# A causal convolution in 64x32 TensorE tiles, eight at once, with a band read as a Toeplitz matrix from one line of taps

## The chip, the cores and the metric

One core of one Trainium2 chip. The metric is the device time of one execution in microseconds, the median of several runs. Each run carries a state, since executions can be slower when the granted clock is lower.

## The reference

A lightweight convolution (eight heads of 24 channels, seven taps each, causal) over 8 x 4160 tokens of 192 channels, then a maxout feed-forward layer:

```python
w = softmax(weight)                              # 8 heads x 7 taps
out[b, s, h, :] = sum_k w[h, k] * x_pad[b, s + k, h, :]      # 6 zero rows ahead of x
h = maximum(maximum(out @ w1, out @ w2), out @ w3)           # 192 -> 768
y = h @ w_out                                                # 768 -> 192
```

## The kernel before

The convolution runs on TensorE. For a chunk of tokens and a head, x (tokens on partitions, 32 channels) is the stationary operand, and a band matrix of the head's taps moves past it. The tokens are cut in 65 blocks of 512; block 64 consists of the eight last 64 tokens of the sequences. Convolutions run four blocks ahead of the feed-forward layer (L285 is its first layer, L319 its second). All code below is cut; `...` marks it.

```python
BAND_W = 128 + PAD        # PAD = 6
CHK = P - PAD             # 122 output tokens from 128 rows

def load_x(t):            # SyncE; consecutive full chunks go in one DMA
    ...
        nc.sync.dma_start(out=xf[0:rlen0, i:k + 1, :], in_=src)

# band: zeros to DRAM, taps scattered over a diagonal, read back, then transposed by two copies
nc.scalar.dma_start(out=Rd[:], in_=zero[:])
...                       # exp, sum, reciprocal, 7 multiplies on 128 partitions
nc.scalar.dma_start(out=bass.AP(... ap=[[BW + NHEAD, P], [1, KW * NHEAD]]), in_=taps...)
nc.scalar.dma_start(out=bandc..., in_=Rd[:])
...
def conv(t):
    for (q, b, row_lo, rlen, lo, hi, cc) in chunks_of[t]:
        for h in range(NHEAD):
            g = h % 4
            ...
            nc.tensor.matmul(G[h // 4][32 * g:32 * g + 32, lo:hi],
                lhsT=x16[0:rlen, q, cb:cb + 32], rhs=band[0:rlen, h, cc:cc + hi - lo],
                start=True, stop=True, tile_position=(0, 32 * g))
...
for t in range(AHEAD):    # start-up: four blocks
    conv(t); evac(t, 0); evac(t, 1)
    repack(t)             # 24-channel heads to dense rows: 10 or 20 small DMAs
    load_x(t + 3); cast_x(t + 3); double(t)   # (under conditions, cut)
    ...
```

The softmax here doesn't subtract the row's maximum and nothing guards it: scores larger than these inputs give would overflow.

## Time and profile before

| | before |
|---|---|
| median (3 runs) | 514.97 us (514.89 to 515.39) |
| span of the profiled run | 513.0 us |
| first, second, fifth, sixth convolution start | 24.68, 26.65, 46.30, 54.36 us |
| period of the loop, from one convolution to the next | 7.046 us |
| first to last matmul of a full block's convolution | 476 ns, 40 pairs of weight load and matmul |

Two more matter afterwards. The first is from the page's list of DMA queues (packets, megabytes, share of the DMA engines' time), the second from its groups of instructions (count, busy us and mean ns, then idle time just before the group and what ended it):

```profile
q8 instruction: 70, 1.15, 1.0%
...
L285 PE MATMUL lq<-yd,wd 64*128 64x512 f16 x1170 | 317.3, 378 | 0.4 <-DVE h L290 0.3
```

The reader sees 70 packets of 16 KB (1.15 MB / 70) that carry instructions, and a first layer that waits 0.4 us in all. TensorE executes 8906 loads and 8906 matmuls, so one packet stands for about 17,812 / 70 = 254 of them.

### The profile page before, as it was taken

How to read it: one execution, taken by the hardware profiler on the slowest of the kernel's cores; microseconds unless marked ns; L12 is line 12 of the kernel's file. 1: busy time of each engine (PE TensorE's matmuls, PEld its weight loads, DVE VectorE, ACT ScalarE, POOL GpSimd, SP SyncE). 2: the span in 40 equal slices, each digit the busy share in tenths (PEclk: the TensorE clock that was granted, in tenths of full speed). 3: DMA queues.
4: the chain of work that ended last, by engine and by line, in shares of the span. 5: the costliest groups of instructions: out<-in, count | busy, mean ns of one | idle time of the engine just before them, and what ended most of it. 6: DMA issues, size and time to landing. Idle time of an engine off the chain costs nothing.

```text
span 513.0 us, 21247 instructions
## 1 busy us (share of the span) xinstructions
PE 470.8 (92%) x8906; PEld 322.7 (63%) x8906; DVE 335.4 (65%) x542; ACT 355.6 (69%) x654; POOL 143.4 (28%) x205
## 2 busy tenths in 40 slices
PE   0084999999999999999999999999999999999993
PEld 0082666666666666666666666666666666666893
DVE  1321676767776777777677767677776777676772
ACT  1132777777777777777777777777777777777661
POOL 1131322333223323223332233322233322323213
PEclk9996999999999999999999999999999999999998
DMA  7825566777666666677666666666677766655412
GB/s 176 215 78 133 139 195 194 198 190 196 176 178 168 186 170 181 186 196 194 194 178 186 188 183 162 171 185 181 195 202 194 190 175 192 172 148 145 123 66 63
DMA packets 65752, 87.72 MB, mean 171 GB/s; under 512 B 7593, under 2 KB 51305, under 8 KB 65657
## 3 DMA queue, kind: packets, MB, share of 16 engines
q1 hardware_dynamic: 54648, 47.36, 33.7%
q0 software_dynamic: 10224, 38.28, 27.6%
q8 instruction: 70, 1.15, 1.0%
q10 hardware_dynamic: 784, 0.72, 0.5%
q14 instruction: 26, 0.20, 0.1%
HBM read 34.93 MB, written 25.85 MB: 118 GB/s over the span
## 4 chain that ended last, share of the span: by engine, by line
PE 88%; DMA 7%; ACT 1%; SPq 1%; ACTq 1%; POOL 1%; issue 0%; DVE 0%; POOLq 0%
PE lp L285 48%; PE po L319 31%; PE G L222 7%; PE lq L285 2%; DMA xf<-in_x_dram 2%; DMA Rd<-taps 2%; DMA bandc<-Rd 1%; DMA Rd<-zero 1%; SPq L265 1%; ACTq L261 1%; POOL out_dram L338 1%; DMA yd<-ys 1%; ACT band L187 1%; ACT ys L238 0%; DVE h L290 0%
## 5 line engine op out<-in xcount | busy, mean ns | idle before, releaser
L290 DVE TENSOR_TENSOR h<-r,lq 128x512 f16<-128x512 f16 x390 | 268.1, 687 | 140.7 <-ACT r L289 140.7
L285 PE MATMUL lq<-yd,wd 64*128 64x512 f16 x1170 | 317.3, 378 | 0.4 <-DVE h L290 0.3
L285 PE MATMUL lp<-yd,wd 64*128 64x512 f16 x1170 | 317.3, 379 | 0.0
L289 ACT ACTIVATE r<-lp 128x512 f16<-128x512 f32 x390 | 232.9, 597 | 110.0 <-PE lq L285 95.1
L319 PE MATMUL po<-wo,h 64*128 64x192 f16 x3120 | 204.4, 243 | 0.4 <-DVE h L290 0.4
L319 PEld LDWEIGHTS <-h 64*128 64x128 f16 x3120 | 152.0, 94 | 58.6 <-DVE h L290 0.6
L285 PEld LDWEIGHTS <-wd 64*128 64x128 f16 x2340 | 110.0, 94 | 48.8 <-issue 3.4
L333 POOL DMA_DIRECT2D out_dram<-o x64 | 49.2, 768 | 240.5 <-DVE o L324 171.2
L238 ACT CAST ys<-G 128x512 f16<-128x512 f32 x130 | 75.4, 583 | 16.4 <-DMA yd<-ys 14.3
L319 PE MATMUL po<-m,yd 64*128 64x192 f16 x780 | 84.7, 243 | 0.0
L133 POOL CAST x<-xf 128x960 f16<-128x960 f32 (+3 forms) x88 | 68.3, 792 | 35.2 <-DMA xf<-in_x_dram 35.2
L222 PEld LDWEIGHTS <-x 128*32 128x32 f16 (+2 forms) x2624 | 36.9, 98 | 59.4 <-issue 45.8
L222 PE MATMUL G<-band,x 128*32 128x122 f16 (+3 forms) x2624 | 43.5, 213 | 33.3 <-DVE band L186 24.7
L324 DVE TENSOR_TENSOR o<-a,po 128x384 f32<-128x384 f32 x130 | 71.1, 547 | 1.7 <-ACT a L323 1.7
L323 ACT COPY a<-po 128x384 f32<-128x384 f32 x130 | 61.8, 476 | 2.0 <-PE po L319 2.0
L319 PEld LDWEIGHTS <-yd 64*128 64x128 f16 x780 | 47.6, 94 | 14.8
L272 POOL DMA_DIRECT2D yd<-yd x33 | 18.1, 548 | 87.0 <-DMA yd<-ys 42.2
L187 ACT COPY band<-bandc 128x536 f16<-128x536 f16 x1 | 2.6, 2559 | 17.4 <-DMA bandc<-Rd 17.4
L183 DVE TENSOR_TENSOR wd<-ws,w3s 128x768 f16<-128x768 f32 x3 | 2.7, 952 | 12.1 <-DMA w3s<-in_moe_w_dram 12.1
L205 PE MATMUL pm<-wos,w3t 128*128 128x192 f32 x24 | 6.3, 443 | 0.0
L205 PEld LDWEIGHTS pm<-wos,w3t 128*128 128x128 f32 x24 | 6.0, 275 | 0.1
L200 DVE COPY w3t<-pt 128x384 f32<-128x384 f32 x3 | 1.7, 555 | 4.3 <-PE pt L198 4.3
(20 smaller groups left out, 20.1 us busy)
## 6 DMA issues: line engine op xcount, KB each, us to landing
out_dram<-o POOLq DMA_DIRECT2D x64, 384.0 KB, 4.0
xf<-in_x_dram SPq DMA_DIRECT2D x48, 480.0 KB
yd<-yd POOLq DMA_DIRECT2D x31, 384.0 KB, 5.9
yd<-ys SPq DMA_DIRECT2D x186, 48.0 KB
xf<-in_x_dram SPq DMA_DIRECT2D x16, 384.0 KB
yd<-ys SPq DMA_DIRECT2D x62, 32.0 KB
ws<-in_moe_w_dram SPq DMA_DIRECT2D x2, 576.0 KB
w3s<-in_moe_w_dram SPq DMA_DIRECT2D x2, 576.0 KB
```

What stands on the lines that cost most here:

```text
L133: nc.gpsimd.tensor_copy(out=x16[0:rl, q0:q1, :], in_=xf[0:rl, q0:q1, :])
L205: nc.tensor.matmul(ps[:], lhsT=w3t[:, j, P * i:P * (i + 1)], rhs=wos[:, j, :], start=(j == 0), stop=(j == NJ - 1))
L222: nc.tensor.matmul(G[h // 4][32 * g:32 * g + 32, lo:hi], lhsT=x16[0:rlen, q, cb:cb + 32], rhs=band[0:rlen, h, cc:cc + hi - lo], start=True ...
L238: nc.scalar.copy(out=slots[g][:, i, NBLK * k:NBLK * k + N], in_=convs[t][i][:, 0:N])
L272: nc.gpsimd.dma_start(out=dense[g][HALF:P, :, w], in_=dense[g][0:HALF, :, w])
L285: nc.tensor.matmul(ps[i][:, 0:N], lhsT=wd[row, c, P * j:P * (j + 1)], rhs=y[row, c, NBLK * k:NBLK * k + N], start=(c == 0), stop=(c == NC ...
L289: nc.scalar.activation(out=r[:, 0:N], in_=ps[0][:, 0:N], func=AF.Relu)
L290: nc.vector.tensor_max(out=hs[t][:, j, 0:N], in0=r[:, 0:N], in1=ps[1][:, 0:N])
L319: nc.tensor.matmul(ps[s // 2, i][:, s % 2, :], lhsT=a, rhs=b, start=first, stop=last)
L323: nc.scalar.copy(out=a[:], in_=ps[s // 2, 0][:])
L324: nc.vector.tensor_add(out=outs[t][:, s - 1:s + 1, :], in0=a[:], in1=ps[s // 2, 1][:])
L333: nc.gpsimd.dma_start(out=out[g0:g0 + n, :].rearrange("(s p) c -> p s c", p=P), in_=ob[:])
```

## The change

Its intent: use all of the array. A 128x32 tile with 128 rows of tokens has four positions; a 64x32 tile has eight, the two row halves working on two halves of the block. A tile then gives 58 tokens, so a block needs 80 pairs instead of 40. The band becomes a read with a step of one element per partition out of a single line of zero-padded taps in DRAM, and the matmul reads it backwards. The diff, cut to its core:

```diff
-BAND_W = 128 + PAD
-CHK = P - PAD
+HALF = P // 2
+CHK = HALF - PAD
+BAND_W = HALF + PAD
+VLEN = HALF + BAND_W - 1
 ...
+        for half, chunks in enumerate(chunks_of[t]):     # two x loads a block, 64 partitions each
 ...
+                nc.sync.dma_start(out=xf[r0:r0 + rlen0, i:k + 1, :], in_=src)
 ...
-    nc.scalar.dma_start(out=Rd[:], in_=zero[:])
-    ... (taps on 128 partitions, scattered write, read back, two copies)
+    nc.vector.tensor_mul(out=line[:, :, HALF - 1:HALF - 1 + KW], ...)
+    nc.scalar.dma_start(out=lined[:], in_=line[:].rearrange("o h v -> o (h v)"))
+    for i in range(2):
+        nc.scalar.dma_start(out=band[HALF * i:HALF * (i + 1), :, :],
+            in_=bass.AP(tensor=lined[:].tensor, ..., ap=[[1, HALF], [VLEN, NHEAD], [1, BAND_W]]))
 ...
-        for (q, b, row_lo, rlen, lo, hi, cc) in chunks_of[t]:
-            for h in range(NHEAD):
+        for q in range(NQMAX):
+            for hg in range(2):
+                for g in range(4):
+                    for i in range(2):
+                        rhs = bass.AP(tensor=bd.tensor, offset=bd.offset + c1,
+                                      ap=[list(bd.ap[0]), [-1, hi - lo]])
+                        nc.tensor.matmul(G[i][32 * g:32 * g + 32, hg, w0:w0 + hi - lo],
+                            lhsT=x16[r0:r0 + rlen, q, cb:cb + 32], rhs=rhs,
+                            start=True, stop=True, tile_position=(r0, 32 * g))
```

## The prediction

> **What bounds the kernel now.** I read the page first: busy time, slices, chain of work.
>
> ```profile
> PE 470.8 (92%) x8906; PEld 322.7 (63%) x8906; DVE 335.4 (65%) x542; ACT 355.6 (69%) x654; POOL 143.4 (28%) x205
> PE   0084999999999999999999999999999999999993
> PE 88%; DMA 7%; ACT 1%; SPq 1%; ACTq 1%; POOL 1%; issue 0%; DVE 0%; POOLq 0%
> PE lp L285 48%; PE po L319 31%; PE G L222 7%; PE lq L285 2%; DMA xf<-in_x_dram 2%; DMA Rd<-taps 2%; DMA bandc<-Rd 1%; DMA Rd<-zero 1%; SPq L265 1%; ACTq L261 1%; POOL out_dram L338 1%; DMA yd<-ys 1%; ACT band L187 1%; ACT ys L238 0%; DVE h L290 0%
> ```
>
> From slice 5 on TensorE never rests: the view of stretches gives 401.60 us busy of 401.60 between 61.4 and 463.0 us. No other engine is above 77% there, so every nanosecond of the convolution's stretch (L222) is paid in full. The loop's period is 7.05 us (one convolution starts at 202.35, the next at 209.40). One of them in the timeline of TensorE:
>
> ```profile
> 202.04 0.38 PE L285 MATMUL lp<-yd,wd 64*128 64x512 f16 x1
> 202.04 0.38 PE L285 MATMUL lq<-yd,wd 64*128 64x512 f16 x1
> 202.35 0.65 PE L222 MATMUL G<-band,x 128*32 128x122 f16 x40
> 202.93 0.39 PE L285 MATMUL lp<-yd,wd 64*128 64x512 f16 x1
> 202.93 0.39 PE L285 MATMUL lq<-yd,wd 64*128 64x512 f16 x1
> ```
>
> Consecutive 512-column matmuls start 0.21 us apart, so the array is free at 202.25; the convolution holds it until 202.93: **0.68 us a block**. By single starts in the trace that is 92 ns before the first matmul, 476 ns from the first to the last of 40, and 102 ns to the next L285. Within the 476 ns, four column tiles start within 3 to 10 ns of each other, then every tile takes its next matmul 53 ns later (122 columns); the last groups, of 24 columns, are 28 ns apart.
>
> Outside the loop there is a start-up of some 46 us, bound by something else:
>
> ```profile
> 1.46 5.78 DMA Rd<-zero
> 7.32 9.38 DMA Rd<-taps
> 16.72 6.53 DMA bandc<-Rd
> 23.27 2.57 ACT band L187
> 25.88 0.96 PE G L222 x24
> ...
> 27.95 0.87 ACTq L261
> ...
> 33.32 1.08 ACT ys L238 x2
> ```
>
> Here the reader sees the band made by three DMAs in a row and a copy, then ScalarE issuing seven repack DMAs before it can evacuate the next block. SyncE's issues follow, until the fifth convolution starts at 46.3.
>
> **What the Trainium skill says.** "TensorE: Matmul & The Clock Gate", Part 3 (Packing small matmuls): tiles run concurrently, at about 4 ns per further tile. The trace agrees for a burst (3 to 4 ns). The same page, Back-to-back issue gap: about 25 ns is the least from start to start, however few columns. The trace has 28 ns at 24 columns, so 58 columns cannot go faster than about 28 ns per group. "TensorEngine Tiling (Array Packing)", Key Properties: a change of tiling mode drains TensorE. The 92 ns ahead and 102 ns behind agree, and the change still switches twice. "Runtime: NRT & Kernel Launch", Instruction fetch mechanics, puts the sequencer's issue floor at about 20 cycles an instruction, 17 ns at the 1.2 GHz that the TensorE page gives for it. The trace is faster and the measurement decides: see the next paragraph.
>
> **The one place that already runs dense small matmuls.** The last block (eight rests of 64 tokens) has 64 matmuls of 64 columns. Timeline of TensorE's weight loads, two windows:
>
> ```profile
> 470.09 0.12 PEld L222 LDWEIGHTS <-x 70*32 70x32 f16 x8 [0.42 <-issue]
> ...
> 470.36 0.30 PEld L222 LDWEIGHTS <-x 70*32 70x32 f16 x26
> ```
>
> Less the 0.093 us of one load, the first eight start 3.6 ns apart, but the 26 later ones (0.30 - 0.093)/25 = **8.3 ns** apart, with the same regularity (8, 8, 9 ns) in the single starts; each is followed by one matmul. The four tiles could have gone at 28 ns per four pairs (7 ns each), and do at first. After about 34 pairs they fall to the 8.3 ns. I read this as the rate at which pairs of weight load and matmul reach the array once a small stock is used up: pairs 7 ns apart against 8.35 ns over 34 pairs means a stock of 34 x 1.35 / 8.35 = 5.5 pairs. Before the change this never shows in full blocks, where 40 pairs take 476 ns, 12 ns each.
>
> **The change part by part.**
>
> 1. Full blocks. Each half of 256 tokens goes in 4 x 58 + 24, five chunks, for two halves and eight heads: 80 matmuls and 80 weight loads instead of 40. Columns alone would be ten groups of eight tiles at 28 ns: 280 ns instead of 476, a gain of 0.19 us. But 80 pairs at 8.35 ns, less the stock of 5.5, take 74.5 x 8.35 = 622 ns. The arrays' eight tiles want a pair every 28/8 = 3.5 ns and get one every 8.35. With the drains unchanged (perhaps 6 ns more behind) a block costs 146 + 6 = **0.15 us more**. Sixty full blocks (4 to 63) lie in the loop: +9.1 us.
> 2. Last block: each 64-token rest is cut in 58 + 6, twice the pairs (128): 64 x 8.35 = +0.5 us. Its 16 small casts on GpSimd (some 0.35 us each, twice as many as before) have a 7 us period to hide in.
> 3. Reading the band backwards and from 64 partitions: no run shows its rate. If it halved the column rate, a group would want 51 ns, still under the 8 x 8.35 = 67 ns of supply, so it costs nothing extra here.
> 4. Start-up. The 268 KB of zeros (5.78 us), the scattered taps (9.38) and the two band copies (1.4 and 2.6 us, side by side) go. In their place are a memset, exponential, sum, reciprocal and one multiply on a single partition, one write of 2128 bytes, and two Toeplitz reads. The exponential can run at about 3.5 us (its table load ends at 3.1), so the line is ready at about 4.5. Small DMAs on ScalarE's queue took 4 to 6 us from issue to first packet while the weights stream in, and about 1.5 us to report; so I estimate the line landed at about 11, the band at 18 to 22, against 25.84 before. The first convolution moves up 4 to 7 us. Against that, SyncE issues two x loads a block in place of one, some 0.4 us each, in the row of issues that leads to the fifth convolution: about 1 us back. Net **-4.7 us**, range -1.5 to -8.
> 5. Evacuation: the same two copies of 128x512 elements, now as 2x256. ScalarE is at 77% in the loop; no change. DMA bytes for x are the same (640 rows a block), the descriptors too.
>
> Sum: 515.0 + 9.1 + 0.5 - 4.7 = 519.9. I shade this to **519** for the chance that supply is a little better with steadier instructions.
>
> **Rivals.** (a) *The array sets the pace*: the 8.3 ns is an artefact of tracing, or of the last block's shape (a wait at every eighth load). Then a block gains 0.19 us: 515 - 60 x 0.19 - 4.7 = 499. For it: the first pairs do go at 3.5 ns, and four column tiles scaled well. Against it: the spacing is equally even at loads with and without a wait, and the profiled execution took 514.83 us against 514.97 unprofiled, though this tests one block only. I give it 0.12. (b) *The start-up gain is hidden*: x of block 1 is cast only at 22.4-23.4, and the bulk loads hold the DMA engines until then; with only 1 us gained, 523. (c) *The start-up gain is full*, 8 us: 516.5. (d) *64-partition x loads are slower* and the loop begins to wait for x: GpSimd's waits for xf would reappear in the loop and the time pass 525. Prefetch is two blocks deep and the DMA engines are at 67%, so this is unlikely: 0.06.
>
> **Range and chances.** With supply the bound, (b) and (c) span 516 to 523. I widen it for an error of 1 ns a pair (80 ns x 60 = 4.8 us) and for a part of (a): **512 to 525**. Faster than 504.7 needs (a): 0.12. Slower than 525.3 needs a slower supply without the start-up gain, or (d): 0.09. Within 2%: 0.79.
>
> **What would show the steps right or wrong.** In the changed trace: convolution matmuls counted 80 a block, some 0.73 us from the first to the next L285 (0.58 now), weight loads 8.3 ns apart over most of it; period 7.2 us; TensorE still without rest; the fifth convolution at about 41.5. A stretch of 0.4 us and a period of 6.86 would prove (a). A stretch well above 0.75 us would mean that backward reads or row tiles cost by themselves. TensorE waits in the loop for GpSimd's casts would mean (d). A fifth convolution near 46 would mean (b).

## The result, and the profile after

The changed kernel took **549.63 us** (median of 4 runs, 545.32 to 550.65), the kernel before 515.18 beside it: a ratio of 1.0651, 95% interval 1.0592 to 1.071. A ratio is the mean time of one kernel's fast runs over that of the other's of the same rounds, so not quite the ratio of the medians quoted. The prediction of 519 us, and its range of 512 to 525, failed.

From the page of the kernel after, the lines that answer to those of before (L296 is now the first layer, L330 the second, L234 the convolution):

```profile
PE 490.7 (90%) x11530; PEld 341.9 (62%) x11530; DVE 334.1 (61%) x535; ACT 351.0 (64%) x653; POOL 143.6 (26%) x197
PE   0085799999999989999999998999999999997993
...
q8 instruction: 90, 1.47, 1.2%
...
PE 83%; SPq 6%; DMA 5%; issue 3%; POOL 1%; ACTq 1%; ACT 1%; DVE 0%; POOLq 0%
...
L296 PE MATMUL lq<-yd,wd 64*128 64x512 f16 x1170 | 320.9, 381 | 3.3 <-issue 3.0
```

TensorE is no longer solidly busy: its row of slices has 8s where before it had 9s, and a 7 near the end. Nothing in the loop fills its place; the chain has 3% "issue", time in which the engine waited for nothing that the profile shows. 5248 more instructions of TensorE brought 20 more instruction packets (23,060 / 90 = 256 loads and matmuls a packet).

The view of waits (what TensorE waited for: us in total, times, longest) makes it plainer. First before, then after; the tile loads at the very start are left out:

```profile
PE G L222 <- POOL x L133: 7.7, 2, 6.5
```

```profile
PE G L234 <- POOL x L141: 18.9, 6, 9.5
...
PE po L330 <- issue: 3.6, 6, 1.3
PE lq L296 <- issue: 3.0, 1, 3.0
PE lp L296 <- issue: 2.8, 2, 1.6
PE G L234 <- issue: 1.4, 2, 1.1
```

There are two new kinds of loss: 11 us more of waiting for GpSimd's casts of x, in the start-up and in the last convolution, and 11 waits for "issue", 10.8 us together, that before had none of. One of these, 1.1 us, ends at 41.07 in the start-up; the other ten, 9.7 us, lie in the loop. The loop's loss of 15.9 us below is larger: the ten periods with such a wait lose 13.5 us in all, since slower stretches follow the long waits, and the other periods lose 2.4 us, up to 0.3 us each, mostly inside a convolution. No run isolates the cause of these 2.4 us.

Where the 34.1 us between the two spans (547.1 - 513.0) lie, by the starts of the convolutions in the traces:

| stretch | before | after | difference |
|---|---|---|---|
| start to sixth convolution (start-up) | 54.36 | 56.56 | +2.2 |
| 59 usual periods of the loop | 59 x 7.046 | 59 x 7.194 | +8.7 |
| what the loop took beyond its usual periods | 0.0 | 440.36 - 59 x 7.194 | +15.9 |
| last convolution's start to the end | 42.9 | 50.2 | +7.3 |

**An undisturbed convolution.** Timeline of TensorE in the kernel after (start, us, and the group of instructions):

```profile
149.97 0.38 PE L296 MATMUL lp<-yd,wd 64*128 64x512 f16 x1
...
150.28 0.80 PE L234 MATMUL G<-band,x 64*32 64x58 f16 x80
151.01 0.39 PE L296 MATMUL lp<-yd,wd 64*128 64x512 f16 x1
```

It holds the array 0.73 us (151.01 - 150.28), as predicted. The single starts of this group in the trace, in ns from the first, show more than the predicted even spacing:

```
pairs 1-8     0   3   6  10  13  16  20  23
pairs 9-16   39  42  45  48  52  56  58  61
...
pairs 29-36  99 102 106 110 120 154 225 233
pairs 37-40 241 250 258 266
... every 8, 8 or 9 ns to pair 80 at 616
```

Some 30 pairs go at the array's pace, about 27 ns per group of eight. Then comes a hole of about 115 ns (from 110 to 225), and every later pair takes 8.3 ns.

**The waits for issue.** A gap in the single starts of TensorE's instructions, beside the packets of the instruction queue that were under way:

```
gap of TensorE           packet on the instruction queue
122.16, 0.63 us          120.04, took 1.30 us
139.29, 1.57 us          138.13, took 1.30 us
198.12, 1.61 us          196.99, took 1.33 us
```

These are three of the nine gaps over 0.5 us in the loop. Each begins while a packet moves or up to 0.95 us after its end, and each ends 1.2 to 1.6 us after that end. "Runtime: NRT & Kernel Launch", Instruction fetch mechanics, says that instructions are fetched in blocks of 16 KiB, 256 instructions, and that crossing a block is "mostly hidden". Before the change it was always hidden. Now a block that holds a whole convolution is used up in 3.9 us, where it took at least 6.1 before. These are estimates, from placing the block ends so that each block has exactly one packet. The longest gap (59.80 to 63.13) is also followed by some 4 us of half speed: consecutive first-layer matmuls start 0.42 us apart, not 0.21.

**The start-up.** Timeline of SyncE's DMA issues, before and then after:

```profile
7.64 0.38 SPq L171 DMA_DIRECT2D wos<-in_moe_w_out_dram  x1
8.07 2.89 SPq L122 DMA_DIRECT2D xf<-in_x_dram  x2
...
33.93 7.31 SPq L265 DMA_DIRECT2D yd<-ys  x10
41.35 1.02 SPq L122 DMA_DIRECT2D xf<-in_x_dram  x2
```

```profile
17.48 0.42 SPq L178 DMA_DIRECT2D wos<-in_moe_w_out_dram  x1
22.11 4.58 SPq L128 DMA_DIRECT2D xf<-in_x_dram  x4
...
34.62 7.37 SPq L276 DMA_DIRECT2D yd<-ys  x10
42.10 2.98 SPq L128 DMA_DIRECT2D xf<-in_x_dram  x4
```

The first convolution did move from 24.68 to 17.68. But x of blocks 1 and 2 is now loaded at 22.11 instead of 8.07, so the second convolution starts later than before (28.34), and x of block 4 is loaded no earlier (42.10 against 41.35), behind ten repack issues of 0.74 us. The late load has to do with the compiled program: the DMA issues of SyncE and ScalarE use eight semaphores in turn, and in the trace such an issue waits until the DMA that last used its semaphore has landed. With other DMAs in the row, w_out's load came to wait for a weight load (11.8 us in the view of SyncE's waits), and the x loads for repack DMAs (6.2 us).

**The end.** SyncE's issue of the last block's x, then TensorE:

```profile
486.13 12.40 SPq L128 DMA_DIRECT2D xf<-in_x_dram  x16
```

```profile
496.92 0.54 PE L234 MATMUL G<-band,x 64*32 64x58 f16 x33
...
501.95 0.23 PE L234 MATMUL G<-band,x 12*32 12x6 f16 x15 [1.52 <-POOL x L141]
502.12 0.60 PE L296 MATMUL lp<-yd,wd 64*128 64x512 f16 x1
```

Sixteen loads at 0.78 us each arrive one by one, so the convolution takes 5.1 us instead of 0.5. After that the matmuls run at half speed until about 507.4.

### The profile page after: what moved, and what is told of

It is laid out like the page before. It is cut to its first block, busy times and chain, and to the rows that moved or that the text cites. A ratio compares the mean times of both kernels' runs of the same rounds, so it can differ in the third digit from the quotient of the medians.

```text
span 547.1 us, 26597 instructions
## 1 busy us (share of the span) xinstructions
PE 490.7 (90%) x11530; PEld 341.9 (62%) x11530; DVE 334.1 (61%) x535; ACT 351.0 (64%) x653; POOL 143.6 (26%) x197
## 4 chain that ended last, share of the span: by engine, by line
PE 83%; SPq 6%; DMA 5%; issue 3%; POOL 1%; ACTq 1%; ACT 1%; DVE 0%; POOLq 0%
PE lp L296 42%; PE po L330 28%; PE G L234 8%; PE lq L296 4%; SPq L276 3%; SPq L128 2%; DMA band<-lined 2%; DMA xf<-in_x_dram 1%; DMA yd<-ys 1%; SPq L272 1%; ACTq L272 1%; POOL out_dram L349 1%; DMA lined<-line 1%; ACT r L300 0%; POOL x L141 0%
## 5 line engine op out<-in xcount | busy, mean ns | idle before, releaser
L296 PE MATMUL lq<-yd,wd 64*128 64x512 f16 x1170 | 320.9, 381 | 3.3 <-issue 3.0
L296 PE MATMUL lp<-yd,wd 64*128 64x512 f16 x1170 | 321.1, 382 | 2.8 <-issue 2.8
L330 PE MATMUL po<-wo,h 64*128 64x192 f16 x3120 | 208.9, 244 | 3.2 <-issue 2.7
L330 PEld LDWEIGHTS <-h 64*128 64x128 f16 x3120 | 156.4, 95 | 60.3 <-issue 5.7
L296 PEld LDWEIGHTS <-wd 64*128 64x128 f16 x2340 | 115.0, 95 | 54.8 <-issue 12.5
L344 POOL DMA_DIRECT2D out_dram<-o x64 | 49.2, 768 | 233.8 <-DVE o L335 199.6
L234 PE MATMUL G<-band,x 64*32 64x58 f16 (+2 forms) x5248 | 56.3, 190 | 38.1 <-POOL x L141 18.9
L234 PEld LDWEIGHTS <-x 64*32 64x32 f16 (+1 forms) x5248 | 48.7, 89 | 65.7 <-issue 37.4
L330 PE MATMUL po<-m,yd 64*128 64x192 f16 x780 | 86.2, 244 | 0.8 <-issue 0.8
L141 POOL CAST x<-xf 128x960 f16<-128x960 f32 (+1 forms) x80 | 68.7, 862 | 57.9 <-DMA xf<-in_x_dram 56.2
L330 PEld LDWEIGHTS <-yd 64*128 64x128 f16 x780 | 48.5, 95 | 15.9 <-issue 1.3
L349 POOL DMA_DIRECT2D out_dram<-o x8 | 4.2, 537 | 0.8 <-DVE o L335 0.8
```

The source lines that it names most:

```text
L141: nc.gpsimd.tensor_copy(out=x16[r0:r0 + rl, q0:q1, :], in_=xf[r0:r0 + rl, q0:q1, :])
L234: nc.tensor.matmul(G[i][32 * g:32 * g + 32, hg, w0:w0 + hi - lo], lhsT=x16[r0:r0 + rlen, q, cb:cb + 32], rhs=rhs, start=True, stop=True, t ...
L296: nc.tensor.matmul(ps[i][:, 0:N], lhsT=wd[row, c, P * j:P * (j + 1)], rhs=y[row, c, NBLK * k:NBLK * k + N], start=(c == 0), stop=(c == NC ...
L330: nc.tensor.matmul(ps[s // 2, i][:, s % 2, :], lhsT=a, rhs=b, start=first, stop=last)
L344: nc.gpsimd.dma_start(out=out[g0:g0 + n, :].rearrange("(s p) c -> p s c", p=P), in_=ob[:])
```

## The experiments

Edits are against the kernel named; line counts are of the essential lines. "Excess" is the loop's time beyond 59 undisturbed periods of that kernel, from the profiled run.

### before_twice: as many pairs, none of the new tiles

```diff
 (before)
-        for (q, b, row_lo, rlen, lo, hi, cc) in chunks_of[t]:
+        for (q, b, row_lo, rlen, lo, hi, cc) in chunks_of[t] * 2:
```

> The kernel before, with every convolution done twice (same result): 352 matmuls and weight loads a block, as many as in the changed kernel, but in four column tiles of 122 columns and with the old x loads. Common to all theories: about 0.49 us more a block for 60 blocks and 0.5 us in the last, 515 + 30 = 545 us. Instruction theory (TensorE now and then runs out of fetched instructions, because a page of 256 lasts only 4 to 5 us where a convolution falls into it): gaps of 0.4 to 3 us at page ends also here, 7 to 15 us in all, 552 to 560 us. Rival (the stalls come from eight row tiles or from x loads of 64 partitions): none of them, 544 to 547 us.

Correct; 553.59 us (552.42 to 558.82), ratio 1.0754, 95% interval 1.0698 to 1.081 (the second pair of numbers after a ratio is this interval below, too). The convolution took 956 ns, the period 7.526, and the waits for issue appear in this kernel too, with its old tiles, old band and old loads (view of TensorE's waits):

```profile
PE G L222 <- issue: 2.3, 2, 1.3
PE lp L285 <- issue: 1.9, 2, 1.3
PE po L319 <- issue: 0.6, 1, 0.6
```

So more instructions a block are enough to bring them. The excess is 5.8 us, though, not 15.9: the number of instructions is not all of it.

### before_newband: the band alone

In the kernel before, the new line of taps, one Toeplitz read over 128 partitions and the backward moving read; tiles unchanged.

```diff
 (before; the band's construction is replaced as in the change)
+                rhs = bass.AP(tensor=bd.tensor, offset=bd.offset + BAND_W - 1 - cc,
+                              ap=[list(bd.ap[0]), [-1, hi - lo]])
-                    rhs=band[0:rlen, h, cc:cc + hi - lo],
+                    rhs=rhs,
```

> The kernel before with the new way to make the band alone (one line of taps, one Toeplitz read, moving operand read backwards), x loads as before. First convolution at about 18 us, not 24.7. If the start-up gain was lost to the row of SyncE's issues (the load of w_out waits until earlier loads have landed, because the band's transfers have taken other places in the row of semaphores), the second convolution is still at 26 to 28 us and the time 513 to 517 us. Rival: it was lost to the doubled x loads; then here the fifth convolution comes at 40 to 42 us and the time is 509 to 511 us. Reading backwards costs nothing: 476 ns from the first to the last of 40 matmuls.

Correct; 513.07 us (512.98 to 513.18), ratio 0.9949, 0.993 to 0.9969. The first convolution comes at 18.15, 6.5 us earlier, the fifth at 44.71, only 1.6 us earlier; w_out's load is issued at 18.12, when the band lands. The convolution takes 476 ns, exactly as with the forward read. This part of the change is a gain of half a per cent by itself.

### last: one cast instead of sixteen

```diff
 (after)
-                row_lo = max(0, S + o - PAD)
+                row_lo = max(0, min(S + o - PAD, SEQ - HALF))
```

The last block's six-token chunks then have 64 rows like all others, and GpSimd casts the block at once.

> The changed kernel with the last block's six-token chunks read from the batch's last 64 rows, so that its 16 casts become one. Theory (the last block's casts hold TensorE for 5 us and its clock then falls): its convolution takes about 1.1 us instead of 5.1, no half clock after it, 549.6 - 6 = 543.5 us. Rival (the end is slow through fetch stalls or stores): 548 to 550 us.

A miss: 552.33 us (547.13 to 556.73; the run of 556.73 is slow, and the three fast ones have a median of 549.5), ratio of the fast runs 1.0677, 1.0602 to 1.0751. The convolution itself shrank to 1.25 us but waited longer, for the one cast that needs all sixteen loads:

```profile
491.24 13.01 SPq L128 DMA_DIRECT2D xf<-in_x_dram  x16
```

```profile
507.71 1.43 PE L234 MATMUL G<-band,x 64*32 64x58 f16 x128 [5.82 <-POOL x L141]
```

Not the casts but the row of issues ahead of them holds the last block up. (In this run the wait stands before the convolution, so it counts in the loop's excess of 26.5 us; without it some 21 are left.)

### four_tiles: both halves from the same 64 partitions

Wrong result (relative error 0.68): `r0 = 0` for both halves, so four tiles do the work of eight.

> The changed kernel with both halves read from partitions 0 to 63, so that only four tiles work (wrong result on purpose; same instructions, waits and columns). Theory (pairs of weight load and matmul arrive every 8.35 ns): 617 ns from the first to the last of 80 matmuls, as with eight tiles. Rival (row tiles or their banks disturb one another): less, down to the 560 ns that 20 groups of four need at 28 ns; if the eight tiles helped at all, more than 617 ns.

546.75 us, a single run. The convolution takes 663 ns, 46 more than with eight tiles. The first 33 pairs go 7 ns apart (225 ns / 32), the pace of four tiles; then come gaps of up to 27 ns; from pair 37 on two pairs take 16.7 ns, so 8.3 ns each, as with eight tiles. Eight tiles help only in the first 30 or so pairs. After that the number of tiles does not matter, so the array does not set the pace there. The excess is 16.1 us, though no convolution uses the second row half.

### half_pairs: eight tiles, forty pairs

```diff
 (after; wrong result on purpose, the other four heads get a copy)
-            for hg in range(2):
+            for hg in range(1):
```

> The kernel after with only the first four heads computed (40 pairs of weight load and matmul a block instead of 80, same eight tiles, same band, same x loads); the other heads' slots get a copy of the same data, so the result is wrong on purpose. Theory (two instruction costs: pairs beyond the first 32 go at 8.35 ns, and pages of instructions that are used up in under about 4.5 us make TensorE wait for the next page): 32 x 3.3 ns + a hole of about 110 ns + 8 x 8.35 ns = about 285 ns from first to last convolution matmul, and the waits at page ends in the loop, 16 us in the kernel after, go to about 0 to 2 us because a block has as many instructions as in the kernel before. Period about 6.86 us; total about 515 - 60 x 0.19 + 2 (start-up) + 7 (last block's 16 loads stay) = 511 to 516. Rival 1 (row tiles, backward reads or the x loads by 64 partitions cause the waits in the loop): the waits of 0.6 to 3.3 us stay in the loop, total 525 or more. Rival 2 (each pair costs the same 7.7 ns throughout): about 300 to 310 ns for 40 pairs, no hole.

511.87 us (2 runs), relative error 0.75. The convolution took 282 to 283 ns (285 expected from 32 fast pairs, the hole and eight slow ones), the period is 6.860. The excess is 2.8 us, a little over the 2 expected; 0.9 of it is a wait for a doubling DMA (yd<-yd). One line of waits for issue is left:

```profile
PE lp L296 <- issue: 0.3, 1, 0.3
```

Tiles, band and x loads are those of the kernel after, and the loss of 15.9 us is nearly gone. The rival that blames row tiles, backward reads or the x loads' shape alone falls.

### last4: four loads for the last block

```diff
 (after, with the edit of `last`)
+        if len(blocks[t]) > 1:
+            for half, chunks in enumerate(chunks_of[t]):
+                for m in range(2):      # first and second chunk of four sequences in one DMA
+                    src = bass.AP(..., ap=[[D, HALF], [SEQ * D, len(chunks) // 2], [1, D]])
+                    nc.sync.dma_start(out=xf[HALF * half:HALF * (half + 1), m:len(chunks):2, :], in_=src)
```

> The kernel after with the last block's x read by 4 DMAs in place of 16: every second chunk begins 64 rows before the end of its sequence, so all chunks have 64 rows, and the chunks of four sequences go in one DMA; one cast in place of 16. Theory (the row of 16 issues of about 0.8 us each on SyncE delays the last block's x, TensorE idles 5 us and comes back at half clock): x is there before the loop reaches the last convolution, that convolution takes about 1.2 us with no wait, no half clock, and the end from the last convolution's start is about 43 to 44 us in place of 50.2. Total 5 to 7 us under the kernel after, 542 to 545, ratio to before about 1.052 to 1.058 (the waits for instructions in the loop stay at 15 to 20 us). Rival (the half clock or the last convolution's wait has another cause, such as instruction fetch or the many small matmuls): the gap before or in the last convolution stays, total 548 to 552.

Correct; 546.32 us (544.66 to 549.54), ratio 1.0585, 1.0532 to 1.0638. Both lines are as hoped:

```profile
491.17 2.72 SPq L122 DMA_DIRECT2D xf<-in_x_dram  x4
```

```profile
502.31 1.42 PE L244 MATMUL G<-band,x 64*32 64x58 f16 x128
```

No wait stands behind the second line, and from here to the end are 43.7 us in place of 50.2. The end of the kernel after's profiled run is thus explained: 6.5 us of its 7.3. The median fell by 3 us, less than the 5 to 7 expected; the profiled run (547.78 us) has an excess of 21 us in the loop against 15.9.

### before_newband_pool: the band's DMAs from GpSimd

The four small DMAs of `before_newband` are issued with `nc.gpsimd.dma_start`.

> The kernel before with the new band (one line of taps, Toeplitz read, backward moving read), its four small DMAs issued on GpSimd's queue instead of ScalarE's. Theory (in the earlier run with the new band, SyncE's loads of w_out and of x of blocks 1 and 2 waited for the band because DMA issues share a few semaphores in rotation, and that ate most of the band's gain): the w_out load is issued near 8 us again as in the kernel before, x of block 1 is cast some 4 to 5 us earlier than the 27 us of that run, second convolution at about 22 to 24, fifth convolution at about 41 to 43 in place of 44.7, total 509.5 to 511.5. Rival (the start-up behind the band is set by something else, ScalarE's row of issues or the weights' transfer): second convolution and fifth move under 1 us, total 512.5 to 513.5.

A miss: 515.96 us (515.05 to 516.89), ratio 0.9996. w_out's load came forward, to 8.98, but the x load of block 1 now waited until 23.90, for a repack DMA (14.5 us in the view of SyncE's waits). GpSimd's own casts were late too: x of block 0 is cast at 16.45, behind the band's issues. Which DMA an issue waits for is a matter of the whole row.

### extra_ldw: a second weight load

```diff
 (after, with the edit of `last`)
+                        nc.tensor.ldweights(x16[r0:r0 + rlen, q, cb:cb + 32], tile_position=(r0, 32 * g))
                         nc.tensor.matmul(
```

> The kernel after with one more weight load ahead of each convolution matmul, the same weights (so the same result), and the last block's second chunks read from the last 64 rows. It tells apart what the 8.35 ns per pair are. Theory A (a cost per instruction, 4.2 ns each): after the first 64 instructions (here 21 triples) a triple takes 12.5 ns, so the convolution takes 21 x about 4 + a hole of 110 + 59 x 12.5 = about 930 ns. Theory B (a cost per weight load, the matmul free beside it): a triple takes 16.7 ns, about 1180 ns. Theory C (a cost per matmul, the load free beside it): a triple takes 8.35 ns, about 690 ns or less. In all three the waits at page ends grow, since a page of instructions then covers less time: over 20 us in the loop.

828.46 us, a single run, correct. All three theories missed: the convolution took 3942 ns. The single starts are instructive all the same. The first 20 triples go 5 ns apart, then a hole (16, 64, 110 ns), then one triple each 64 ns. Twenty triples are 60 instructions, thirty-odd pairs are 60 to 68: the stock is counted in **instructions**, about 64. "Advanced Engine Details and Errata", Engine Queue Depths, gives TensorE a queue of 64, and the runs agree. Why a triple then costs 64 ns and not some 13 is not explained here, so this run does not say what the 8.3 ns are made of. The waits for issue, expected to grow past 20 us, are absent from its loop. That miss fits the account: with so slow a convolution, any 256 consecutive loads and matmuls in its loop take at least 4.7 us.

### before_newband_early: x of blocks 1 and 2 first

```diff
 (before_newband)
     load_x(0)
+    load_x(1)
+    load_x(2)
 ...
-    load_x(1)
-    load_x(2)
```

> The kernel before with the new band (line of taps, Toeplitz read, backward moving read, issued by ScalarE as in the earlier run with it), and SyncE's loads of x of blocks 1 and 2 moved ahead of the weights in the program. Theory (what ate the band's gain is that these x loads were issued only at 22 us, behind DMAs on whose semaphores they wait, so block 1 was cast only at 27): x1 and x2 are cast before 15 us, the second convolution follows the first by 1 to 3 us (near 20), the fifth starts at 38 to 42 in place of 46.30 in the kernel before, total 507 to 511. Rival (the row of repack DMA issues on ScalarE and SyncE, or the weights for the merged matrix, set the fifth convolution): fifth at 44 or later, total 512 to 514.

A miss: 514.79 us, ratio 0.9981, 0.996 to 1.0001. The casts are done by 11.5 and the second convolution follows the first at once, but the first comes only at 21.91 and the fifth at 46.97. w_out's load now waits 17.7 us for a repack DMA and goes at 26.02.

### last4_early: the same for the changed kernel

> The kernel after with the last block's x in 4 DMAs (as in the earlier run) and the loads of x of blocks 1 and 2 ahead of the weights. Same theory of the start-up: fifth convolution at about 43 in place of 48.74 (4 to 7 us earlier), so 538 to 542 with the waits for instructions unchanged at 16 to 24 us and the longer convolution unchanged. If it comes at 544 to 547, the start-up's x loads are not what cost it.

Correct; 540.97 us (538.77 to 543.64), ratio 1.0504, 1.0459 to 1.0548. The time is in the expected range, but not for the expected reason: the fifth convolution starts at 46.46, not at 43, and the sixth at 54.96. Against `last4`'s profiled run that is 1.9 us from the start-up; 7.3 us is a smaller excess (13.7 us), which varies between runs.

### no_x: no loads of x in the loop

Blocks 3 to 63 use the x of blocks 0 to 2 again; wrong (relative error 0.92). TensorE's program is the same.

> The kernel after without x loads in the loop: blocks 3 and on, but the last, use the x of blocks 0 to 2 again, so the result is wrong on purpose; instructions of TensorE are the same. It tells apart why a page of instructions comes late. Theory A (its 16 KB packet waits behind the data of x on the DMA engines): the time from the moment that TensorE enters a page to the landing of the next falls well under its median of about 2.8 us, and the waits in the loop fall from 16 us to under 5. Theory B (the delay is set by when the fetch is asked for, or by the other traffic of repack and stores): waits of 10 to 20 us stay.

528.19 us, a single run. The excess is 1.8 us. In the view of waits only one for issue is left, and by its start (40.55) it belongs to the start-up:

```profile
PE G L238 <- issue: 0.6, 1, 0.6
```

Estimated from the block ends as above, the next block of instructions lands 3.2 us after the current one is entered in 9 cases of 10, 3.7 at the most; in the kernel after these are 4.6 and 6.2. The shortest block lasts 3.9 us in both. The move of one packet itself takes 1.1 us in this run and 1.2 in the kernel after (medians); it is its start that is earlier. So the waits need both: blocks of instructions used up in about 4 us, and DMA traffic that delays the packets.

### forward: the band reversed once

> The kernel after with the band reversed once by a VectorE copy and read forward by the matmuls. If the backward read costs nothing (as predicted): first to last convolution matmul 617 ns as in the kernel after, first 32 pairs 3.3 ns apart, then 8.35 ns. If it slows a matmul: well under 617 ns. Start-up about 1 us later, total within 4 us of the kernel after.

Correct; 540.93 us, a single run. First to last matmul: 617 ns, as with the backward read. The total is 9 us under the kernel after's median, beyond the 4 expected; of the 8.0 us between the two profiled spans, 4.0 are a smaller excess (11.9 us), 5.1 a shorter end, and the start-up takes back 1.1, as expected. The convolution part of it is clear: the backward read costs nothing.

### before_swap, before_newband_swap, before_newband_early_swap: x loads ahead of the repacks

```diff
 (before, before_newband, before_newband_early: in the start-up)
-        repack(t)
         if t + 3 <= AHEAD + 1:
             load_x(t + 3)
+        repack(t)
```

> The kernel before, with the loads of x of blocks 3 to 5 issued ahead of the repack DMAs of the block before them in the start-up. Theory (the fifth convolution waits for x of block 4, whose load stands behind 17 repack issues of about 0.74 us on SyncE): that load is issued at about 33 in place of 41.35, the fifth convolution comes at 40 to 42 in place of 46.30, total 509 to 511. Rival (the first layer's dense input, that is the repacks themselves, is what TensorE then waits for): TensorE's idle time only moves behind the fifth convolution, total 513 to 516.

> The same change of order on top of the kernel before with the new band. Same theory: the load of x of block 4 at about 32, fifth convolution at about 39 to 41 in place of 44.71, total 507 to 510, the fastest so far (513.07 without the change of order). Rival: 512 to 514.

> New band, x of blocks 1 and 2 ahead of the weights, and x of blocks 3 to 5 ahead of the repacks. If the x loads were all that stood between the band and the loop: 506 to 509. If the late w_out load (26 us in the earlier run with the early x) or the repacks bound it: 510 to 514, no better than before_newband_swap.

All three results are correct, and the rival wins each time, though the times lie 0.8 to 2.2 us above its ranges: 516.79, 514.88 and 516.21 us, ratios 1.0035 (1.002 to 1.0049), 1.0001 (0.9983 to 1.0018) and 1.0033 (1.0006 to 1.006). The fifth convolution does move, to 39.11, 40.10 and 38.67. The idle time goes elsewhere: in before_swap TensorE waits before the sixth (first line), for a cast that stands on GpSimd behind the doubling DMA of blocks 2 and 3, which needs their repacks (second and third; the view names an x load, which uses the same semaphore as an earlier repack, but the last of the repacks landed at 51.47, just ahead of the doubling):

```profile
53.64 1.05 PE L222 MATMUL G<-band,x 128*32 128x122 f16 x40 [3.92 <-POOL x L133]
```

```profile
52.07 0.53 POOL L272 DMA_DIRECT2D yd<-yd  x1 [7.78 <-DMA xf<-in_x_dram]
52.59 1.00 POOL L133 CAST x<-xf 128x960 f16<-128x960 f32 x1
```

The sixth convolution starts at 53.64, 52.92 and 53.23, against 54.36 before and 52.59 in before_newband, and the seventh comes another 1.7 to 2.8 us later than a period would have it. By these traces the start-up is bound by its 27 repack issues on SyncE and what follows them, not by any one x load.

### before_twice_x64: x loads of 64 partitions

> The kernel before with every convolution done twice, and each x load split in two DMAs of 64 partitions, as the kernel after has them. Theory A (the shape of the x loads makes pages of instructions come later): waits in the loop 14 us or more, where the unsplit one had about 7, total 560 or more. Theory B (the shape does not matter; the kernel after waits more because its pages, of 4.0 us at the shortest, are used up sooner than the 4.2 to 4.3 us of this kernel): waits 4 to 9 us, total 552 to 557.

559.52 us (2 runs, 556.86 and 562.18), ratio 1.0866, 1.0805 to 1.0928. The profiled run has an excess of 7.9 us, where before_twice has 5.8, and a sixth convolution 2.2 us later (59.45). The excess is as theory B expects, the time nearer to theory A: the split loads cost something at the start, and at most a small part of the loop's excess. Inconclusive on the rest.

## Why the prediction was wrong

**Step 1, full blocks: right in size, wrong in one detail.** Predicted 622 ns, 0.73 us of array time and +9.1 us; measured 617 ns, 0.73 us and +8.7 us. Rival (a), the array as the bound, is refuted by the 8.3 ns that eight and four tiles share. The "stock of 5.5 pairs" is a right sum and a wrong picture. The queue's worth of some 64 instructions goes at the array's pace; then TensorE waits until the slow pace has caught up. In before's last block, which the prediction read, the slow pace begins after 32 pairs, not 34: weight load 33 starts 225 ns after the first. After the change load 34 starts at 231 ns. Both, and all later loads, lie on one line, load n at about 8.33 n - 51 ns. So the hole is not a cost of its own, and the prediction's rule, 8.35 x (n - 5.5), gives nearly this line: 488 ns for 64 pairs, 288 for 40 and 622 for 80, where 485, 282 to 283 and 617 were measured. That it came out is no luck, but only the single starts show why.

**The step that failed most: "TensorE still without rest".** The sum had no term for fetching instructions, though the same reading of supply led up to it: I asked how fast pairs get from the queue to the array, and not whether the queue's own source keeps up. The loop's loss is 15.9 us, half of the miss: 9.7 us of waits for instructions, 3.8 us more in the same periods, and 2.4 us elsewhere whose cause is not shown. Shown: it comes with instructions (before_twice), goes with them at the same tiles and loads (half_pairs), and goes with the x traffic (no_x). Open: why before_twice has 5.8 us where the changed kernel and its variants with 80 pairs and all x loads have 12 to 21. It is not the eight tiles (four_tiles: 16.1). Its blocks of instructions last at least some 4.2 us instead of 3.9, which fits, but no run isolates it.

**Step 2, last block: +0.5 predicted, +7.3 measured.** The casts do hide, as predicted. What does not is SyncE's row of 16 issues of 0.78 us; its doubling from 8 is in the diff, and the prediction counted only the casts. Shown by last4 (43.7 us to the end), with last as the control that removes only the casts. The size varies with where these issues fall: forward, four_tiles and no_x, with the same 16 loads, need 45.2 to 46.6 us from there to the end, so 2.2 to 3.6 us more than before. Against these last4 would have gained only 1.5 to 2.9 us: 7.3 is the size in one profiled run.

**Step 3, the backward read: right.** Zero, by before_newband (476 ns) and forward (617 ns).

**Step 4, start-up: -4.7 predicted, +2.2 measured.** The band landed at 17.7, a little before the predicted 18 to 22, and the first convolution moved by 7 us. (A DMA's 1.5 us to report was read too long: from its last packet to the next step, before's trace has 0.6 to 1.1 us.) The error was to pass this gain on to the fifth convolution. Rival (b) named a hidden gain, but with the wrong keeper (bulk loads): it is the row of SyncE's issues, with their shared semaphores and 27 repacks. Of its 6.5 us gained, before_newband keeps 1.8 at the sixth convolution; in the changed kernel, whose x loads stand in that same row with two issues a block, it is a loss. That the split does this is not isolated, but in before_twice_x64 it alone put the sixth convolution back by 2.2 us. Bringing x loads forward moved the sixth convolution up by 1.9 us at the most, and in one kernel back by 2.3.

**Step 5 and rival (d):** in the loop TensorE does not wait for GpSimd's casts until the last block, so the loads by 64 partitions are in time. They are at most a part of what delays instructions.

Summed: 8.7 + 15.9 + 7.3 + 2.2 = 34.1 us, the whole difference of the spans. The best correct version found is before_newband: the band of the change without its tiles, 0.5% under the kernel before.

## What to carry to other kernels

Splitting matmuls to fill more tiles sped them up here only while the pairs fitted TensorE's queue: beyond some 32 in a row they came 8.3 ns apart, with four tiles as with eight. In an unrolled kernel count the instructions per microsecond as well: a stretch that uses 256 of them in 4 us can run dry when DMA traffic is dense, and the profile shows it only as "issue". Before crediting a start-up gain, follow it through the row of DMA issues to the engine that ends the start-up, and count the issues of the odd last block, for each cost 0.7 to 0.8 us here.

## What the Trainium skill lacked or had wrong

- "Runtime: NRT & Kernel Launch", Instruction fetch mechanics: crossing a block of instructions is called mostly hidden, since issue is slower than the fill. Here it was not: 9.7 us of waits in the loop and 13.5 us with what followed them, of 547; gaps of up to 3.3 us, with blocks used up in about 4 us (estimate) under DMA traffic, and no such wait in the loop without the x loads.
- The same section gives TensorE a store of 128 KiB, eight such blocks. In the runs it did not seem to act as a reserve: TensorE went on 1.2 to 1.6 us after the end of a single packet, as if it had no block left. No run shows how full the store was.
- The same section's issue floor of about 20 cycles an instruction (17 ns in the prediction, an estimate with the 1.2 GHz of "TensorE: Matmul & The Clock Gate"): pairs of weight load and matmul were sustained at 8.3 ns, 4.2 ns an instruction, and the first 60 or so instructions went at 3 to 4 ns a pair. The section makes no exception for these two; that TensorE page does (Wait — 56ns, not 53.3ns?), listing them as not using this sequencer.
- "Advanced Engine Details and Errata", Engine Queue Depths: the depth of 64 agrees (20 triples, or 30 to 34 pairs, at the array's pace). The page lacks what comes when it is used up: later pairs 8.3 ns apart, the first of them some 225 ns after the start, so a hole of about 115 ns where the array had been quick.
- No page that bears on the change gives the cost of two weight loads in a row to the same tile: 64 ns for a load, a load and a matmul once the queue was used up.
